# K loads on a second queue in a planned attention and feed-forward kernel

## The chip, the core and the metric

The kernel runs on one core of one Trainium2 chip. A core has five engines that each work through their own list of instructions in order: TensorE (PE in the profile) multiplies matrices, ScalarE (ACT) evaluates functions such as exp and tanh, VectorE (DVE) does elementwise arithmetic, GpSimd (POOL) does casts here, and SyncE (SP) only issues transfers. They meet through semaphores. Transfers between the chip's memory and the core's on-chip memory (SBUF) run on 16 DMA engines; SP, ACT and POOL each have a queue into them. Matmul results land in PSUM, eight banks of 2 KB per partition.

The metric is the time of one execution on the device, in microseconds (us), as the median of several runs.

## The reference

Eight batches of eight heads, 576 positions, head size 64: blockwise causal attention with blocks of 64, and then, on its 4608 rows of 512, a feed-forward layer with the activation h·sigmoid(beta·h).

```python
scores = scale * q @ k.T                      # per batch and head, 576 x 576
scores = where(pos_i // 64 >= pos_j // 64, scores, -1e9)
attn = softmax(scores)
x = (attn @ v).transpose(0, 2, 1, 3).reshape(4608, 512)
h = x @ w_in                                  # 512 -> 2048
g = h * (1 / (1 + exp(-beta * h)))
out = g @ w_out                               # 2048 -> 512
```

All inputs and the output are float32. The kernel multiplies in bf16 and f16.

## The kernel before, in words

**Attention.** The work is cut into 32 units, `u = 4*b + c`: batch `b`, pair of heads `c`. A unit needs Q and K with the head dimension on the partitions (`QKT`), so Q and K are loaded (`ST`), cast to bf16 on POOL (`QKn`) and transposed. For batches 0 and 1 a pair's Q and K come in small loads (L606), and PE transposes them (L622, copied out by DVE at L630). From batch `QB = 2` on, all of a batch's Q is one load and all of its K another (L641, 1.18 MB each), each into one of the two big buffers of class `S8`; POOL casts them in four pieces each (L653), and two DMA transposes (L660), one for each two pairs, write `QKT`. Then PE forms the transposed scores (L692), two heads at once on two halves of the array ("row" mode), ACT takes exp into `E` (L706, L718), DVE clears the masked corners (L712, L714), PE multiplies by V with a column of ones beside it (L744, "AV" below), and DVE divides by the sum (L756, L763). The result `xq` is transposed into `xT`, by PE and a copy for batches 0 to 2 (L783, L791, L793), by DMA from batch 3 on (L770). V comes in six loads a batch (L536, L539) into one buffer `Vs` and is cast by POOL (L562).

**Feed-forward.** It goes by nine blocks of 512 rows. For each of 16 columns of tiles, PE multiplies `xT` by `w_in` (L955, four matmuls a group), ACT takes tanh (L965) and DVE combines them into `gT` (L969). Block 0 then multiplies by `w_out` plainly (L991, 64 matmuls of 512 columns). The other blocks use Strassen's seven products (L885). ACT and DVE move the results to `ost`, and ACT issues the stores (L910, L1012).

**Weights.** POOL issues four loads of `w_in` (L490) and four of `w_out` (L495), which cast on the way. All four loads of `w_out` wait for the V of batch 1.

**What sets the order.** All of this is written as operations with a cost, dependences, buffers and a priority, and the class `Plan` orders them before the program is built: it simulates the five engines, PSUM banks and buffers, and the order in which its operations start becomes each engine's list of instructions. On the chip only the order is left, with the waits that `assign` derives. The plan's time for a load is `xfer` (what it would take alone), shared among queues that are active at once in proportion to `pkt`. It knows two queues before: "H" for all that SP and ACT issue, in one line, and "S" for POOL (L104 to L112). A list `seq` (L805 to L816) gives the loads on SP an order, through `after`; most of them are `lazy`, held back while over 3 us of load are queued.

Where PE would be idle in the plan's first 50 us, the plan puts in matmuls on a constant (fills, L511 in full mode, L513 as pairs in row mode). They read nothing that the kernel needs and keep PE busy. Their planned cost is 215 ns for the first 12 and 110 ns after.

Of the kernel before, what the change touches and what calls it, by code (L numbers as in the profile page):

```python
# [4 lines left out]
ACT = mybir.ActivationFunctionType  # L5
# [43 lines left out]
class Plan:  # L49
# [33 lines left out]
    def schedule(self):  # L83
# [20 lines left out]
        rings, left, clock = {"H": [], "S": []}, {"H": 0.0, "S": 0.0}, 0.0  # L104
        told, late = None, []

        def speeds():
            if rings["H"] and rings["S"]:
                h, w = rings["H"][0].pkt, rings["S"][0].pkt
                both = self.BOTH if clock > self.FIRST else self.BOTH0  # L110
                return {"H": h / (both * (h + w)), "S": w / (both * (h + w))}
            return {"H": 1.0, "S": 1.0}  # L112
# [56 lines left out]
        while nsched < len(self.ops) - len(fill) or pend or rings["H"] or rings["S"] or late:  # L169
# [26 lines left out]
            while progress:  # L196
                progress = False
                for e in engs:
# [62 lines left out]
                    if o.dma is not None:  # L261
                        x = "S" if e == "POOL" else "H"
                        left[x] += o.xfer
                        full = max(0.0, left[x] - self.RING) if e == "SP" else 0.0
                        o.todo = o.xfer
                        if x == "S":
                            at = now + (self.LATE if now > self.FIRST else self.LATE0)
                            late.append((at, o))
                            heapq.heappush(events, at)
                        else:  # L270
                            rings[x].append(o)
                        flow(now)
# [82 lines left out]
def bass_blockwise_causal_attn__then__act_swish_beta_kernel(  # L355
# [10 lines left out]
    with es:  # L366
# [138 lines left out]
        for i in range(NFILL):  # L505
            tf = P.tile("P1")

            def ff(g, e, tf=tf, i=i):
                o = fills[i]
                if o.mode == "full":  # L510
                    return g.matmul(PS[:, tf.slot, 0:256], identB[:], identW)  # L511
                for r in (slice(0, 64), slice(64, 128)):
                    z = g.matmul(PS[r, tf.slot, 0:256], identB[r, r], identW[r, :])  # L513
                return z

            n = 215 if i < 12 else 110
            o = P.op("PE", n, ff, deps=[c2, c4], tiles=[tf], lat=n, mode="full", prio=1e6 + i)
            o.fill = TFILL
            fills.append(o)
# [4 lines left out]
        for b in range(B):  # L524
# [4 lines left out]
            for h0, h1, e, tt in PARTS[b]:  # L529

                vs = []
                for i in tt:
# [10 lines left out]
                    if e == "SP":  # L543
                        o = P.op("SP", 300 + 550 * n, fv, tiles=[ts], xfer=(1400 if b == 0 else 1580) * n,
                                 prio=3.5 + 0.1 * (h0 > 0) if b == 0 else 4 * b + (3.5 if b < 2 else 0.5),
                                 dma=["d_V", h0, 1])
                    else:
# [40 lines left out]
        QKI, QKX = 1000, 5400  # L588
        for u in range(NU):
# [44 lines left out]
            elif p == 0:  # L634

                for w, (nm, src) in enumerate((("Q", q), ("K", k))):
                    if c == 0:
                        ts = whole[w] = P.tile("S8")

                        def fl(g, e, ts=ts, src=src, b=b):  # L640
                            return [g.dma_start(ST[ts.slot][:], src[b].rearrange("h t d -> (h t) d").rearrange(  # L641
                                "(i p) d -> p i d", p=128))]

                        o = P.op("SP", QKI, fl, deps=[o for t in early6 for o in t.users] if b == QB else [],
                                 tiles=[ts], xfer=QKX, prio=u, dma=["d_S8", 0, 1])
                        for i in range(NPAIR):
                            ld[nm, u + i] = o
                    ts, o = whole[w], ld[nm, u]
# [137 lines left out]
            xp = P.op("PE", 5 * 66, fx, deps=nrm, tiles=[tx, px], lat=5 * 66 + 170, mode="full", prio=pr(u)+.5 + 5 * (b < 1))  # L786

# [18 lines left out]
        for b in range(B):  # L806
            for u in range(4 * b, 4 * b + 4):
                for o in (ld["Q", u], ld["K", u]):
# [135 lines left out]
        for r in range(NRC):  # L944
# [37 lines left out]
            for w, d0, d1 in [(w, 0, DM) for w in range(4)]:  # L982
# [5 lines left out]
                for j0, j1 in parts:  # L988
# [12 lines left out]
                    o.after = was  # L1001
# [83 lines left out]
```

## Time and profile before

| | |
|---|---|
| median of 3 runs | 340.45 us (340.06 to 344.98) |
| span of the profiled run | 340.1 us |
| PE busy | 325.4 us (96%) |
| DVE, ACT, POOL busy | 220.9, 211.6, 83.0 us |
| DMA bytes | 53.41 MB, 157 GB/s over the span, 193 to 241 GB/s in most slices of the first 230 us |

The profile's page gives busy time by engine, then the span in 40 slices of 8.5 us with a digit for the busy tenths, then DMA by queue, the chain of work that ended last, and groups of instructions by source line. Beside it stand answers of the trace: the list of waits (who waited for whom, total, times, longest), the timeline (start, length, engine, line, operation, and in brackets the idle time before it and what ended it), and tables of windows. A PE duration is partly modelled, since matmuls are pipelined: eight matmuls of 256 columns follow each other at 109 ns although each is shown with a mean of 273 ns.

### The profile page before, as it was taken

What the parts mean: (1) busy time and instruction counts of PE and PEld (TensorE: products, weight loads), DVE (VectorE), ACT (ScalarE), POOL (GpSimd) and SP (SyncE); (2) the same over time, 40 slices, a digit from 0 to 9 for tenths busy, and PEclk for the clock granted to TensorE, in tenths of its full rate; (3) what the DMA queues carried; (4) which work ended last, traced back from release to release, by engine and by line L of the source; (5) the groups of instructions that cost most, each with busy time, mean ns of one, the idle gap of its engine ahead of it and who ended that gap; (6) DMA issues with size and microseconds to landing.
All of it is one profiled execution on the core that took longest, in us unless ns stands there. A gap on an engine that the chain in (4) does not pass through costs nothing.

```text
span 340.1 us, 7452 instructions
## 1 busy us (share of the span) xinstructions
PE 325.4 (96%) x3104; PEld 205.2 (60%) x3081; DVE 220.9 (65%) x447; ACT 211.6 (62%) x314; POOL 83.0 (24%) x127
## 2 busy tenths in 40 slices
PE   7798999999998999999999999999999999999995
PEld 5366446544685546754665676466656766666684
DVE  4718768479663687547976685657566766666742
ACT  1861993268645886777687747877677545544511
POOL 7665180316414400432035124303000000000000
PEclk9879999999999999999999999999999999999999
DMA  8999899999999595999889979994221200110023
GB/s 218 220 238 234 169 234 241 230 230 227 210 199 227 137 212 115 193 195 213 176 176 206 207 172 242 193 207 116 72 60 22 81 32 33 39 56 31 18 78 123
DMA packets 113313, 53.41 MB, mean 157 GB/s; under 512 B 83568, under 2 KB 112768, under 8 KB 113280
## 3 DMA queue, kind: packets, MB, share of 16 engines
q1 hardware_dynamic: 98432, 39.14, 57.7%
q10 hardware_dynamic: 9280, 9.44, 9.0%
q0 software_dynamic: 5568, 4.36, 8.1%
q8 instruction: 24, 0.39, 0.5%
q14 instruction: 9, 0.07, 0.1%
HBM read 36.71 MB, written 9.44 MB: 136 GB/s over the span
## 4 chain that ended last, share of the span: by engine, by line
PE 83%; ACT 9%; DVE 5%; issue 2%; POOL 0%; POOLq 0%; ACTq 0%
PE PS L955 31%; PE PS L885 28%; PE PS L744 7%; PE PS L692 7%; ACT E L706 5%; PE PS L991 4%; ACT th L965 3%; DVE gT L969 2%; PE PS L511 2%; PE PS L513 2%; PE PS L783 1%; PE PS L622 1%; DVE xq L763 1%; DVE QKT L630 1%; DVE QKn L613 0%
## 5 line engine op out<-in xcount | busy, mean ns | idle before, releaser
L955 PE MATMUL PS<-xT,w_in 128*128 128x512 bf16 x543 | 131.1, 380 | 3.2 <-ACT xT L791 0.4
L965 ACT ACTIVATE th<-PS,beta 128x512 f32<-128x512 f32 x144 | 96.6, 695 | 60.1 <-PE PS L955 59.7
L969 DVE SCALAR_TENSOR_TENSOR gT<-th,PS 128x512 f16<-128x512 f32 x144 | 95.7, 682 | 37.9 <-ACT th L965 37.4
L706 ACT ACTIVATE E<-PS 128x1024 bf16<-128x1024 f32 x93 | 92.0, 1027 | 32.8 <-PE PS L692 32.7
L955 PEld LDWEIGHTS PS<-xT,w_in 128*128 128x128 bf16 x576 | 52.9, 98 | 57.4 <-issue 2.7
L885 PE MATMUL PS<-w_out,gT 128*128 128x256 f16 x512 | 63.9, 273 | 0.3 <-ACT ost L900 0.3
L885 PEld LDWEIGHTS PS<-w_out,gT 128*128 128x128 f16 x512 | 48.6, 98 | 12.4 <-issue 0.4
L653 POOL CAST QKn<-ST 128x640 bf16<-128x640 f32 x48 | 35.7, 744 | 46.8 <-DMA ST<-in_k_dram 25.7
L562 POOL CAST Vn<-Vs 128x640 bf16<-128x640 f32 (+1 forms) x28 | 20.9, 747 | 93.6 <-DMA Vs<-in_v_dram 92.3
L692 PE MATMUL PS<-QKT 64*64 64x64 bf16 (+4 forms) x328 | 37.8, 303 | 0.4 <-ACT E L706 0.3
L744 PEld LDWEIGHTS PS<-Vn,E 128*128 128x128 bf16 x930 | 31.4, 97 | 7.0 <-DVE E L712 1.5
L744 PE MATMUL PS<-Vn,E 128*128 128x65 bf16 x930 | 32.6, 193 | 2.4 <-DVE E L712 1.2
L885 PE MATMUL PS<-OV 128*128 128x256 f16 x256 | 32.1, 273 | 0.0
L900 ACT ACTIVATE ost<-PS 128x512 f32<-128x512 f32 x32 | 19.2, 601 | 20.6 <-PE PS L885 20.2
L692 PEld LDWEIGHTS PS<-QKT 64*128 64x128 bf16 (+1 forms) x328 | 13.6, 97 | 26.8 <-issue 14.3
L885 PEld LDWEIGHTS PS<-OV 128*128 128x128 f16 x256 | 24.3, 98 | 5.8 <-issue 0.4
L763 DVE TENSOR_TENSOR xq<-PS,inv 128x640 bf16<-128x640 f32 x32 | 26.3, 821 | 0.7
L903 DVE SCALAR_TENSOR_TENSOR ost<-PS,ost 128x512 f32<-128x512 f32 x24 | 16.4, 688 | 13.0 <-PE PS L885 8.3
L712 DVE MEMSET E<- 64x64 uint32 x62 | 6.9, 112 | 25.8 <-ACT E L706 24.1
L852 DVE TENSOR_TENSOR OV<-gT 128x1024 f16<-128x1024 f16 x32 | 22.8, 727 | 0.4
L885 PE MATMUL PS<-OV,gT 128*128 128x256 f16 x128 | 15.9, 273 | 0.0
L991 PE MATMUL PS<-w_out,gT 128*128 128x512 f16 x64 | 15.2, 380 | 0.0
(60 smaller groups left out, 175.4 us busy)
## 6 DMA issues: line engine op xcount, KB each, us to landing
out_dram<-ost ACTq DMA_DIRECT2D x36, 256.0 KB, 2.8
Vs<-in_v_dram SPq DMA_DIRECT2D x24, 256.0 KB, 4.9
ST<-in_q_dram SPq DMA_DIRECT2D x8, 288.0 KB, 6.8
ST<-in_k_dram SPq DMA_DIRECT2D x8, 288.0 KB, 6.9
w_in<-in_moe_w_in_dram POOLq DMA_DIRECT2D x4, 512.0 KB, 10.7
w_out<-in_moe_w_out_dram POOLq DMA_DIRECT2D x4, 512.0 KB, 11.7
OV<-in_v_dram SPq DMA_DIRECT2D x4, 256.0 KB, 10.2
Vs<-in_v_dram SPq DMA_DIRECT2D x6, 128.0 KB, 8.0
```

The costliest lines, as they stand in the source:

```text
L562: return g.tensor_copy(Vn[t.slot][:, 0:n, g0:g1, 0:64], Vs[ts.slot][:, 0:n, g0:g1, :])
L653: return g.tensor_copy(QKn[tn.slot][:].rearrange("p a w n -> p (a w n)")[:, 640 * (2 * a + w):][:, 0:640] .rearrange("p (t h d) -> p t h d ...
L692: z = g.matmul(o, QKT[tqk.slot][r, p, 1, 128 * t + y:128 * t + m + y], x)
L706: return g.activation(E3[es_(te)][:, g0, :, :], PS[:, ps.slot:ps.slot + 2, :], ACT.Exp, scale=0.125)
L744: z = g.matmul(o, eblk(te, t, i, h), Vn[Tv.slot][:, t, 2 * c + h, 0:65], start=(t == 0), stop=(t == i))
L763: return g.tensor_tensor(xq[tx.slot][:].rearrange("p i (h d) -> p h i d", h=2), both(pv, 0, 64), x, ALU.mult)
L852: return P.op("DVE", dve_t(SZ * HC / 2), mk(lambda g: g.tensor_tensor(fo(), fx(), fy(), op)), deps=deps, tiles=tiles, prio=prio)
L885: x = g.matmul(PS[:, ps.slot, HM * w:HM * w + HM], fa()[:, j, 128 * w:128 * w + 128], fb()[:, j, :], start=first and w == 0 and j == 0, st ...
L955: z = g.matmul(PS[:, ph.slot, :], w_in[:, c, 128 * j:128 * j + 128], xT[:, c, row % RX:row % RX + RC], start=(c == 0), stop=(c == 3))
L965: return g.activation(th[tt.slot][:], PS[:, ph.slot, :], ACT.Tanh, scale=beta[:, j:j + 1])
L969: return g.scalar_tensor_tensor(out=gT[tg.slot][:, j, :], in0=th[tt.slot][:], scalar=1.0, in1=PS[:, ph.slot, :], op0=ALU.add, op1=ALU.mult)
L991: z = g.matmul(PS[:, po.slot, 0:d1 - d0], gT[tg.slot][:, j, 128 * w:128 * w + 128], w_out[:, j, d0:d1], start=(j == 0), stop=(j == NJ - 1))
```

## The change

From batch 2 on K's load is issued by ACT, so it goes through ACT's queue, where before only the stores were. Q's load stays on SP. Three more things go with it.

- The planner gets a third queue, "A", for what ACT issues; three active queues share by `pkt`. An issue on ACT into a full queue now holds ACT in the plan.
- Loads get times and weights that were read from a trace: V from batch 1 on 1200 in place of 1580 for a full piece, with `pkt` 90 in place of 22 (for batch 0 too); Q and K 5900 in place of 5400, with 72 in place of 22. Fills cost 140 in place of 110 after the first 12.
- Of K's loads of batches 2 to 7, none is in `seq` any more: each may go once Q of its batch has started in the plan, and none is lazy. Q always takes buffer 0 and K buffer 1. The plain products with `w_out` of rows 256 to 511 of block 0 may start, in the plan, only after the last PE transpose of batch 1 (`turn`).

What is computed is the same. Since the order of nearly everything follows from the plan, the lists of all engines change. PE's list in the changed kernel has 29 fills in full mode and 38 half-array ones, against 32 and 68; it changes into row mode 59 times against 56. The last part, from the last AV on, is the same matmuls in the same order.

```diff
-        rings, left, clock = {"H": [], "S": []}, {"H": 0.0, "S": 0.0}, 0.0
+        rings, left, clock = {"H": [], "A": [], "S": []}, {"H": 0.0, "A": 0.0, "S": 0.0}, 0.0
...
         def speeds():
-            if rings["H"] and rings["S"]:
-                h, w = rings["H"][0].pkt, rings["S"][0].pkt
-                both = self.BOTH if clock > self.FIRST else self.BOTH0
-                return {"H": h / (both * (h + w)), "S": w / (both * (h + w))}
-            return {"H": 1.0, "S": 1.0}
+            p = {k: r[0].pkt for k, r in rings.items() if r}
+            both = 1.0 if len(p) < 2 else self.BOTH if clock > self.FIRST else self.BOTH0
+            return {k: p[k] / (both * sum(p.values())) if k in p else 1.0 for k in rings}
...
-                        x = "S" if e == "POOL" else "H"
+                        x = {"POOL": "S", "ACT": "A"}.get(e, "H")
                         left[x] += o.xfer
-                        full = max(0.0, left[x] - self.RING) if e == "SP" else 0.0
+                        full = max(0.0, left[x] - self.RING) if x != "S" else 0.0
...
-            n = 215 if i < 12 else 110
+            n = 215 if i < 12 else 140
...
-                        o = P.op("SP", 300 + 550 * n, fv, tiles=[ts], xfer=(1400 if b == 0 else 1580) * n,
+                        o = P.op("SP", 300 + 550 * n, fv, tiles=[ts], xfer=(1400 if b == 0 else 1200) * n,
                                  prio=3.5 + 0.1 * (h0 > 0) if b == 0 else 4 * b + (3.5 if b < 2 else 0.5),
                                  dma=["d_V", h0, 1])
+                        o.pkt = 90.0
...
-        QKI, QKX = 1000, 5400
+        QKI, QKX = 1000, 5900
...
                         ts = whole[w] = P.tile("S8")
+                        ts.only = (w,)
...
-                        o = P.op("SP", QKI, fl, deps=[o for t in early6 for o in t.users] if b == QB else [],
+                        o = P.op("ACT" if w else "SP", QKI, fl, deps=[o for t in early6 for o in t.users] if b == QB else [],
                                  tiles=[ts], xfer=QKX, prio=u, dma=["d_S8", 0, 1])
+                        o.pkt = 72.0
                         for i in range(NPAIR):
                             ld[nm, u + i] = o
+                        if w:
+                            o.after = ld["Q", u]
...
+            if u == 2 * NPAIR - 1:
+                turn = xp
...
-                for o in (ld["Q", u], ld["K", u]):
+                for o in (ld["Q", u], ld["K", u])[:2 if b < QB else 1]:
...
-                    o.after = was
+                    o.after = was or (turn if w > 1 else None)
```

More of the change, by code (lines that the diff above doesn't have):

```diff
@@ L168, in schedule @@
         fill = [o for o in self.ops if o.fill]
-        while nsched < len(self.ops) - len(fill) or pend or rings["H"] or rings["S"] or late:
+        while nsched < len(self.ops) - len(fill) or pend or any(rings.values()) or late:
             if not events:
```

## The prediction

> **What bounds the kernel now.** I read the page first, then the windows, then the timelines of PE, SP and POOL where PE loses time. The page:
>
> ```profile
> PE 325.4 (96%) x3104; PEld 205.2 (60%) x3081; DVE 220.9 (65%) x447; ACT 211.6 (62%) x314; POOL 83.0 (24%) x127
> ...
> PE   7798999999998999999999999999999999999995
> ...
> ACT  1861993268645886777687747877677545544511
> ...
> DMA  8999899999999595999889979994221200110023
> ```
>
> PE is the bound: 96% busy, and the other engines have room. The DMA engines are nearly full for the first 230 us, but PE hardly waits for them, since feed-forward work fills the time of attention. From 264 us on there is only that work; both kernels have the same matmuls there, in the same order. So a load that lands earlier gains nothing by itself. Only time that PE loses can be won: waits, fills, and changes between array modes. The windows say where it is lost (columns: busy us of PE, PEld, DVE, ACT, POOL with counts, granted clock, DMA share, GB/s):
>
> ```profile
> 17.00:25.00 8.00, 8.00 (x99) 5.07 (x98) 1.36 (x7) 5.64 (x7) 5.23 (x8) 0.74 1.14 240
> 25.00:34.00 9.00, 7.87 (x168) 6.30 (x163) 7.77 (x17) 1.61 (x5) 5.11 (x8) 1.00 1.20 233
> 34.00:52.00 18.00, 17.16 (x136) 7.99 (x131) 12.84 (x27) 17.32 (x27) 9.38 (x13) 1.00 1.00 203
> 52.00:82.00 30.00, 29.71 (x249) 15.09 (x244) 21.05 (x44) 14.90 (x23) 6.35 (x9) 1.00 1.11 233
> 82.00:100.00 18.00, 17.84 (x215) 11.97 (x211) 12.65 (x30) 12.96 (x20) 6.53 (x8) 1.00 1.08 214
> 100.00:130.00 30.00, 28.60 (x275) 16.14 (x267) 19.56 (x47) 22.19 (x34) 8.64 (x12) 1.00 0.88 187
> 130.00:160.00 30.00, 28.84 (x338) 19.53 (x332) 17.12 (x40) 20.18 (x30) 8.64 (x12) 1.00 0.95 181
> ```
>
> PE idles 1.13 us in 25 to 34, 0.84 in 34 to 52, 0.45 in the next two together, 1.40 and 1.16 in the last two. Idle time is not all of it: from 17 to 25 PE is busy without a gap, but with what? DVE works 1.36 us there. The timeline of PE:
>
> ```profile
> 21.31 1.06 PE L513 MATMUL PS<-identF,identB 64*64 64x256 bf16 x16
> 22.31 0.39 PE L692 MATMUL PS<-QKT 64*128 64x64 bf16 x4
> 22.63 0.95 PE L513 MATMUL PS<-identF,identB 64*64 64x256 bf16 x14
> 23.51 0.39 PE L692 MATMUL PS<-QKT 64*128 64x320 bf16 x4
> 23.84 0.84 PE L513 MATMUL PS<-identF,identB 64*64 64x256 bf16 x12
> 24.61 1.98 PE L744 MATMUL PS<-Vn,E 128*128 128x65 bf16 x60
> ```
>
> Fills, and AV of the first two units behind them. POOL's timeline has the casts of their V from 19.12 for 1.50, so done by 20.6. AV stood ready for 4 us behind fills that the plan had put there for a V it expected later. ACT then has 1.61 us of work from 25 to 34, and 17.32 of 18 from 34 to 52: idle first, the limit after.
>
> For K, the timeline of SP and the issues by line:
>
> ```profile
> 40.20 0.75 SPq L641 DMA_DIRECT2D ST<-in_q_dram  x1
> 41.40 4.29 SPq L641 DMA_DIRECT2D ST<-in_k_dram  x1
> 45.74 17.74 SPq L536 DMA_DIRECT2D Vs<-in_v_dram  x4
> 63.53 7.14 SPq L660 DMA_TRANSPOSE QKT<-QKn  x2
> ```
>
> ```profile
> L641 SPq DMA_DIRECT2D ST<-in_q_dram x6: 719/726/751, 40.2 to 200.2; - x6
> L641 SPq DMA_DIRECT2D ST<-in_k_dram x6: 722/4284/4435, 41.4 to 208.0; - x6
> ```
>
> K's issue holds SP for 4.28 us (min/median/max in ns) where Q's takes 0.73: it finds the queue full of Q. V's four issues then hold SP until 63.5, and only then do the transposes go. POOL waits 25.7 us in all for K, six times (the list of waits). PE does not wait for any of it.
>
> [...] the DMA row is full with one load queue and POOL's, [...] No row of before shows two such queues with large loads from SP and ACT; SP and POOL together do: K of batch 2, issued at 41.40, is cast from 59.62 on, with three loads of `w_out` issued meanwhile. [...]
>
> **The change part by part.**
>
> *K's issue on ACT.* SP loses six issues of 4.28 us in the median; no engine but SP was held by them. ACT gains six: at least 0.73 + 0.37 us (Q's issue and the shape move before it, same listing), together 6.6 us, with an empty queue. If ACT's queue were as full as SP's was, 4.3 us each, 26 us. I take the low end: ACT's queue otherwise holds stores of 256 KB, which were issued in 0.38 us even at 174.9, while SP stood in a K issue. ACT is 62% busy, so most of the 6.6 us lie in its idle time; I charge PE a tenth, 0.6 us, with both ends 0 and 3.
>
> *The wait that comes with it.* Each of the six issues waits for POOL's casts of the K before. Behind it in ACT's list stand exp and tanh, and PE waits for those within a few us, as scores and `w_in` products share eight PSUM banks. The list puts the first issue after exps of batch 1, when POOL's last cast (33.88 + 0.82 before) should be just done, and the others one batch's work, some 30 us, apart, while K's casts follow its landing at once. I take 0 and keep 2 us each, 10 in all, for a rival.
>
> *Fewer fills and an earlier AV.* Before, 34 half-array pairs cost 6.1 us in the groups by line, 0.18 each. The pairs planned at 140 are 19. In the timeline, 13 of the old pairs lie before 21 us at about 0.22 (half clock) and 21 after it in 2.65 us; of the new ones 10 lie before (2.2 us in place of 2.86) and 9 after at some 0.15 (1.35 in place of 2.65). That is 2.0 us. One group of scores, 0.4, also moves behind the first AV, which can then start at about 22.3 in place of 24.6. Its V is cast by 20.6, so nothing else holds it. The transposes and scores of batch 1 follow some 4 to 5 us earlier than the 33.7 of before, into ACT's idle stretch, since POOL's list has three of their casts before two issues of `w_in` (1.48 us) that were ahead of them.
>
> How much of it lasts? The next gate is V of batch 1. It was waited for by POOL until 41.9, and K of batch 2 now starts at about 36 and shares with it for its last 5 us: some 3 us later, 44 to 45. Its casts, 0.77 each, follow the first `w_out` issue (0.74), so AV of batch 1 can start at about 46. At the same amount of PE work before had reached 51.35 less 16 matmuls of `w_in` at 0.216, or 47.9. So 1.9 us last if this gate binds, 5 if it doesn't. I take 3.0.
>
> *Fewer waits from 100 us on.* The two windows 100 to 160 idle 2.56 us, of which about 0.2 per 20 us is unavoidable by the later windows, so some 1.4 us are to be had there, and as much may lie in gaps too short for the row. A plan that has its load times from measurement puts work where its inputs really are, and K arrives with Q. I take 1.5 of it, between -3 (new misplacements, since a list is fixed) and +6.
>
> *Three more changes into row mode.* Before a group of scores the trace shows "issue" gaps, 14.3 us in 58 of them, 0.25 each: +0.75.
>
> *`turn`, buffers, `seq`, V's times.* They reorder work that is done anyway; no cost.
>
> Sum: 0.6 - 3.0 - 1.5 + 0.75 = -3.15, so 340.45 goes to **337.3 us**.
>
> **The rivals.** *A, the middle empties too:* with Q and K together, scores never wait, and the start keeps its 5 us: 0 - 5 - 4 + 0.75 = -8, 332.4. For it: 25.7 us of POOL's waits for K. Against: PE is at 99% from 52 to 100 already, and DMA is as full as before. *B, the transfer was hidden anyway:* the start's gain is lost at V of batch 1 and at `w_out`, all of it on full DMA engines: 0.6 - 0.5 - 0.5 + 0.75, or 340.8, no change. For it: the DMA row. Against: before, PE at 24 us waited for its own list, not for a load. *C, ACT is held:* 10 us from POOL's casts, 0.6 for issues, 0.75, with 3 won at the start: +8.4, 348.8, slower. For it: ACT at 17.32 of 18 us just where the first K is issued. Against: POOL is idle three quarters of the time.
>
> **How the numbers follow.** Forecast 0.52, A 0.22, B 0.18, C 0.08. The range from 331.8 to 342.5 holds the forecast with its bounds, A and B, and leaves C and the far end of A. Faster by over 2% means below 333.6: A, and a little of the forecast, 0.23. Slower by over 2% means above 347.3: most of C, 0.06. The rest, 0.71, is within.
>
> **What would show it.** In the changed kernel: the first AV at 22 to 23 us, the half-array fills at about 3.6 us in place of 6.1, and PE's idle time in 25 to 52 smaller than 1.97. K's issues on ACT near 0.73 us, with the wait ahead of them near nothing. K's casts no longer long after Q's. PE's idle time in 100 to 160 below 2.6. The forecast is wrong if ACT stands before a K issue while PE waits for exps, if AV of batch 1 waits for V beyond 48, or if the first scores of batch 2 wait for their transposes by several us.

## The result and the profile after

The changed kernel takes 365.74 us in the median of 4 runs (364.09 to 367.67), the kernel before, beside it, 342.72 (340.06 to 345.20, 4 runs): 1.070 times as long, with a 95% interval of 1.057 to 1.084. The forecast was 337.3, with a range of 331.8 to 342.5. Ratios, here and below, compare only the runs in the faster of the two states that the executions of one kernel fall into, so a ratio can differ from that of the medians beside it. The span of the profiled run grew from 340.1 to 362.3 us. Page of the changed kernel:

```profile
PE 332.3 (92%) x3104; PEld 205.7 (57%) x3048; DVE 218.2 (60%) x447; ACT 211.0 (58%) x320; POOL 82.4 (23%) x127
...
PE   7879959876998999999956999999999999999996
...
PEclk9999969996999999999995999999999999999999
DMA  8999999999999599999799786150231021020023
```

PE's row has three holes: a 5 in the sixth slice, a 7 and a 6 in the ninth and tenth, a 5 and a 6 in the 21st and 22nd. PEclk, the granted clock, drops to 5 or 6 in or just behind each of them. From 200 us on PE has no such hole. The windows (columns as before):

```profile
17.00:25.00 8.00, 6.49 (x121) 4.49 (x117) 3.44 (x12) 4.20 (x6) 5.20 (x8) 1.00 0.98 234
...
34.00:52.00 18.00, 12.99 (x113) 6.79 (x108) 9.68 (x20) 11.14 (x18) 3.77 (x6) 0.91 1.13 220
52.00:82.00 30.00, 26.52 (x206) 13.19 (x199) 15.38 (x33) 9.63 (x15) 10.67 (x15) 0.94 1.16 206
82.00:100.00 18.00, 15.35 (x124) 6.86 (x123) 10.14 (x22) 13.98 (x22) 8.91 (x12) 0.81 1.12 218
100.00:130.00 30.00, 29.08 (x311) 19.35 (x301) 17.29 (x43) 17.08 (x28) 8.64 (x12) 1.00 0.88 187
130.00:160.00 30.00, 29.07 (x324) 17.71 (x315) 19.96 (x45) 22.46 (x34) 6.10 (x8) 1.00 1.06 214
...
180.00:200.00 20.00, 13.16 (x110) 7.56 (x107) 8.89 (x19) 8.59 (x16) 3.22 (x4) 0.74 1.10 211
```

PE's idle time is 5.0 us in 34 to 52 (0.84 before), 3.5 in 52 to 82 and 2.7 in 82 to 100 (0.45 for both before), 6.8 in 180 to 200. The timeline of PE names the waits, in brackets:

```profile
20.13 1.08 PE L747 MATMUL PS<-Vn,E 128*128 128x65 bf16 x30 [0.50 <-POOL Vn L561]
...
49.57 2.65 PE L747 MATMUL PS<-Vn,E 128*128 128x65 bf16 x45 [4.57 <-POOL Vn L561]
...
84.43 1.89 PE L960 MATMUL PS<-xT,w_in 128*128 128x512 bf16 x4 [4.73 <-ACT ost L1011]
...
193.24 1.83 PE L747 MATMUL PS<-Vn,E 128*128 128x65 bf16 x30 [6.84 <-DMA xT<-xq]
```

The first AV stands at 20.13 us instead of 24.61. Most of that distance is not the change: in the profiled execution of before PE had half clock from 14.3 to 21.1 us. h1 below has the list of before on PE, and its profiled execution had no half clock there; its timeline of PE has this AV at 21.17:

```profile
21.17 1.98 PE L744 MATMUL PS<-Vn,E 128*128 128x65 bf16 x60
```

So at full clock the new list gains 1.0 us. With half clock early in both (h2 below has the new list and half clock from 12.1 to 19.0) it gains 2.7, with the AV at 21.93 against 24.61.

Then PE waits 4.6 us for V of batch 1, 4.7 for ACT and 6.8 for a DMA transpose. The timelines of SP and then of ACT show what stood where:

```profile
34.37 3.62 SPq L534 DMA_DIRECT2D OV<-in_v_dram  x1
38.04 1.64 SPq L537 DMA_DIRECT2D OV<-in_v_dram  x2
40.14 0.75 SPq L641 DMA_DIRECT2D ST<-in_q_dram  x1
```

```profile
37.44 0.86 ACTq L641 DMA_DIRECT2D ST<-in_k_dram  x1
...
75.64 0.60 ACT L1011 ACTIVATE ost<-PS 128x512 f32<-128x512 f32 x1 [1.04 <-PE PS L996]
76.50 0.69 ACT L970 ACTIVATE th<-PS,beta 128x512 f32<-128x512 f32 x1 [0.27 <-PE PS L960]
76.50 7.23 ACTq L1017 DMA_DIRECT2D out_dram<-ost  x1
83.78 0.60 ACT L1011 ACTIVATE ost<-PS 128x512 f32<-128x512 f32 x1 [6.59 <-issue]
```

K is issued at 37.44, just ahead of the two last, small pieces of V of batch 1 (38.04). By the trace's landings these took 8.7 us each (2.9 and 2.5 before) and landed at 46.8 and 47.8, K itself at 47.5: the pieces came in together with K, and V was there at 47.8 instead of 41.6. At 76.50 a store's issue stands 7.23 us on ACT, with K, issued at 73.97, ahead of it in the same queue. At 185.13 the transposes of `xT` were issued 0.5 us after K (184.65); they took 8.1 us and landed at 193.2, again behind K (192.7). K's own issue costs what was forecast, and waits for nothing:

```profile
L641 ACTq DMA_DIRECT2D ST<-in_k_dram x6: 712/732/946, 37.4 to 184.7; - x6
L641 SPq DMA_DIRECT2D ST<-in_q_dram x6: 726/732/751, 40.1 to 191.2; - x6
```

**A balance.** The trace records each change of the granted clock. Leaving out the last stretch of each kernel, which begins in the last 2 us of the span or behind it, the changed kernel has half clock in three stretches, 48.7 to 55.5, 82.8 to 89.6 and 188.6 to 198.8 us; before has one, 14.3 to 21.1. Half a clock for t us is counted here as a loss of t/2, an estimate (30 matmuls of an AV took 1.08 us at 20.13 and 1.83 at 193.24). The gaps are those of over 1.5 us between the starts of two matmuls, from 25 us on. Without both, the spans of the kernels that are needed below lie at 333 to 336 us, and at 339 to 340 for two of them:

| kernel | span | gaps | half clock | span - gaps - half clock/2 |
|---|---|---|---|---|
| before | 340.1 | 1.5 | 6.8 | 335.2 |
| after | 362.3 | 17.2 | 23.9 | 333.2 |
| e1, planned anew with K on SP | 350.7 | 6.5 | 10.2 | 339.1 |
| e6, before with the new times | 346.9 | 3.6 | 6.8 | 339.9 |
| h1, list of before, K on ACT | 357.9 | 19.1 | 10.2 | 333.7 |
| h2, list of after, K on SP | 360.4 | 14.3 | 20.5 | 335.9 |
| h3, h1 with stores on POOL | 349.5 | 11.6 | 6.8 | 334.5 |
| b2, list of before, two edits | 335.9 | 1.5 | 0 | 334.4 |

So what the change lost are a few long waits of PE and the half clock behind them: 17.2 + 11.9 = 29.1 us against 4.9. What it won, some 2 us of the rest, is small beside that. e1 and e6 lose more than the table's waits: gaps of 0.6 to 1.5 us add up to 10 to 12 us over the span in the four kernels of the table whose list was planned with the new times, and to 4 to 6 in the others. The experiments ask where the waits come from.

### The profile page after: what moved, and what is told of

It is laid out like the page before. It is cut to its first block, busy times and chain, and to the rows that moved or that the text cites. A ratio compares the mean times of both kernels' runs of the same rounds, so it can differ in the third digit from the quotient of the medians.

```text
span 362.3 us, 7406 instructions
## 1 busy us (share of the span) xinstructions
PE 332.3 (92%) x3104; PEld 205.7 (57%) x3048; DVE 218.2 (60%) x447; ACT 211.0 (58%) x320; POOL 82.4 (23%) x127
## 4 chain that ended last, share of the span: by engine, by line
PE 69%; DVE 6%; SPq 6%; DMA 6%; ACT 4%; POOL 3%; ACTq 3%; issue 2%; POOLq 0%
PE PS L960 28%; PE PS L890 24%; PE PS L747 7%; SPq L534 5%; PE PS L695 5%; PE PS L996 4%; DVE gT L974 3%; ACTq L1017 2%; DMA OV<-in_v_dram 2%; DMA xT<-xq 2%; ACT E L709 2%; DMA Vs<-in_v_dram 1%; DVE xq L766 1%; DVE OV L857 1%; ACT th L970 1%
## 5 line engine op out<-in xcount | busy, mean ns | idle before, releaser
L960 PE MATMUL PS<-xT,w_in 128*128 128x512 bf16 x576 | 143.3, 388 | 5.2 <-ACT ost L1011 4.7
L747 PE MATMUL PS<-Vn,E 128*128 128x65 bf16 x930 | 35.2, 198 | 12.2 <-DMA xT<-xq 6.8
L747 PEld LDWEIGHTS PS<-Vn,E 128*128 128x128 bf16 x930 | 33.5, 101 | 17.8 <-DMA xT<-xq 7.1
L695 PE MATMUL PS<-QKT 64*128 64x512 bf16 (+4 forms) x328 | 37.6, 300 | 2.3 <-ACT E L709 2.0
L695 PEld LDWEIGHTS PS<-QKT 64*128 64x128 bf16 (+1 forms) x328 | 13.5, 96 | 30.1 <-issue 13.8
L759 DVE RECIPROCAL inv<-PS 128x10 f32<-128x10 f32 x32 | 6.9, 217 | 18.9 <-PE PS L747 18.6
L996 PE MATMUL PS<-w_out,gT 128*128 128x512 f16 x64 | 16.3, 395 | 0.0
```

Of the source, the lines that this page charges most:

```text
L695: z = g.matmul(o, QKT[tqk.slot][r, p, 1, 128 * t + y:128 * t + m + y], x)
L747: z = g.matmul(o, eblk(te, t, i, h), Vn[Tv.slot][:, t, 2 * c + h, 0:65], start=(t == 0), stop=(t == i))
L960: z = g.matmul(PS[:, ph.slot, :], w_in[:, c, 128 * j:128 * j + 128], xT[:, c, row % RX:row % RX + RC], start=(c == 0), stop=(c == 3))
L996: z = g.matmul(PS[:, po.slot, 0:d1 - d0], gT[tg.slot][:, j, 128 * w:128 * w + 128], w_out[:, j, d0:d1], start=(j == 0), stop=(j == NJ - 1))
```

## The experiments

There were three theories at first. "One line": loads of SP and ACT move in the order in which they are handed over, while the plan lets them share. "Sharing": they share. "Constants": the new times make a list that fits badly whatever the queue.

### The loads alone

A kernel of loads and stores only: nothing is computed, and most of the output is not written. Each case ran twice in one execution, and the two agree within 0.3 us in each landing.

> Only loads and stores, nothing is computed and most of the output is not written. Twice through five cases, each begun when all before has landed: Q (1.18 MB) from SP and K from ACT at once; K from ACT, then V's two last pieces (64 KB each) from SP; Q from SP, then two stores (256 KB) from ACT; K from POOL, then the pieces from SP; K from ACT, then two stores from ACT. Theory one line: of Q and K at once one lands after some 8 us and the other after 13; the pieces from SP land only with K from ACT, some 8 us after their issue, but after 3 to 5 us beside K from POOL. Theory sharing: Q and K both land after 12 to 13 us, and the pieces after 3 to 5 us in both cases. A store behind K in ACT's own queue is held 3 us or more at its issue under both.

Its timeline (first the case of K and small pieces, then that of K and a store on one queue):

```profile
15.35 0.70 ACTq L81 DMA_DIRECT2D SK<-in_k_dram  x1
16.09 0.20 ACT L82 ACTIVATE w<-w 128x1 f32<-128x1 f32 x1 [0.78 <-issue]
16.39 1.36 SPq L72 DMA_DIRECT2D VS<-in_v_dram  x2
23.91 0.20 ACT L85 ACTIVATE w<-w 128x1 f32<-128x1 f32 x1 [7.62 <-DMA VS<-in_v_dram]
...
43.27 0.70 ACTq L81 DMA_DIRECT2D SK<-in_k_dram  x1
44.02 0.20 ACT L82 ACTIVATE w<-w 128x1 f32<-128x1 f32 x1 [0.78 <-issue]
44.09 4.39 ACTq L87 DMA_DIRECT2D out_dram<-STO  x1
```

Two pieces of 64 KB, handed over by SP 1 us after K on ACT, land 7.2 and 6.7 us later, right behind K (8.0). With K from POOL, and the pieces 2.2 us after it, the same (7.6 and 7.2). Q and K handed over in the same instant share: 11.3 and 13.2 us. A store right behind K on ACT stands 4.39 us in its issue, 4.68 the second time; one beside Q on the other queue 0.36. So "one line" holds for these small pieces behind a load that was already handed over, by POOL too, which neither theory had expected; "sharing" for two handed over together.

This is no rule for all transfers. Two stores that ACT issued 0.0 and 0.4 us after Q on SP landed after 2.5 and 5.2 us, well ahead of Q (8.2). In the kernel before, the first two loads of `w_out` that POOL issued after K of batch 2 landed at 50.8 and 55.6 us, K at 59.6.

### The list planned anew

**e1**: K back on SP and in `seq`; the third queue (for stores), the times and `turn` stay.

```diff
-                        o = P.op("ACT" if w else "SP", QKI, fl, ...
+                        o = P.op("SP", QKI, fl, ...
-                for o in (ld["Q", u], ld["K", u])[:2 if b < QB else 1]:
+                for o in (ld["Q", u], ld["K", u]):
```

> The changed kernel with K of batches 2 to 7 issued by SP again and in the list of loads; the planner's third queue (now for stores alone) and all new times stay, and everything is planned anew. Theory one line (loads that SP and ACT issue are moved in the order of issue, while the plan lets them share, so K on ACT goes ahead of V's last pieces and of later stores): V of batch 1 lands by 42 us, PE has no wait of over 2 us after 40 us, the clock stays full; 335 to 343 us. Theory sharing (K takes a fair third of the DMA engines, and the extra load is what delays V): the same, 335 to 343. Theory constants (the new times and weights give a list that doesn't fit, whatever the queue): 355 or more.

Measured: 352.59 us, ratio 1.035 (1.028 to 1.041). Between the two expectations: with K on SP, over 3% are still lost.

**e6**: before with the new times alone.

```diff
-            n = 215 if i < 12 else 110
+            n = 215 if i < 12 else 140
...
-                        o = P.op("SP", 300 + 550 * n, fv, tiles=[ts], xfer=(1400 if b == 0 else 1580) * n,
+                        o = P.op("SP", 300 + 550 * n, fv, tiles=[ts], xfer=(1400 if b == 0 else 1200) * n,
...
+                        o.pkt = 90.0
...
-        QKI, QKX = 1000, 5400
+        QKI, QKX = 1000, 5900
...
+                        o.pkt = 72.0
```

> The kernel before, K on SP and its plan of one load line, with the changed kernel's load times alone: half-array fill 140 instead of 110, V 1200 with weight 90 instead of 1580 with 22, Q and K 5900 with weight 72 instead of 5400 with 22. Theory 'times': the new times by themselves make a list that fits the loads worse, then 350 to 356, as when K was put back on SP with the rest of the change kept (352.6). Theory 'queue': the new times fit as well as the old ones and only a plan that lets two queues share is wrong: 335 to 344.

Measured: 348.73 us, 1.026 (1.023 to 1.029). The new times by themselves cost 7.8 to 9.9 us, more than "queue" allowed and a little less than "times" asked. Of it the timeline of PE shows one long wait, with 3.4 us of half clock behind it; the rest is in shorter gaps, which were not followed one by one:

```profile
172.46 1.05 PE L887 MATMUL PS<-w_out,gT 128*128 128x256 f16 x8
176.88 1.42 PE L957 MATMUL PS<-xT,w_in 128*128 128x512 bf16 x4 [3.37 <-DMA xT<-xq]
```

These transposes were issued at 167.12, right behind Q (166.35) on SP, and took 9.4 us. In before they are no faster (8.4 us for those behind Q and K of the same batch), but PE's list comes to them later: among its waits there is none for a DMA.

**e7**: before's single line and old times, with K on ACT.

```diff
-                        o = P.op("SP", QKI, fl, ...
+                        o = P.op("ACT" if w else "SP", QKI, fl, ...    # only=(w,), after Q, not in seq
```

> The kernel before with K on ACT alone: issued behind Q as in the change, but planned with the old times, in the old single line with SP's loads, stores too, and ACT charged only for its issue. Theory 'K on ACT costs by itself': stores behind K hold ACT for 3 to 8 us and later small loads wait for K, so 350 to 362 although the plan's times are old. Theory 'plan': with the old times and no sharing between SP and ACT assumed, the list fits: 336 to 345.

Measured: 362.07 us (355.72 to 368.58), 1.048 (1.042 to 1.053). As "K on ACT costs by itself" has it, though in the profiled run ACT was held only 5.8 us in two issues. The larger part were waits of up to 2.6 us between 101 and 124 us, with 20.5 us of half clock, whose cause was not followed further.

**e2** and **e8** give the planner the order that the loads alone showed. e2 puts ACT into SP's line; e8 keeps the three queues and serves, of SP's and ACT's loads, only the one handed over first.

```diff
# e2
-                        x = {"POOL": "S", "ACT": "A"}.get(e, "H")
+                        x = "S" if e == "POOL" else "H"
# e8, in speeds()
+            last = max((k for k in "HA" if k in p), key=lambda k: rings[k][0].start, default=None)
+            if "H" in p and "A" in p:
+                p.pop(last)                 # its speed: 1e-9
...
```

> The changed kernel, K still issued by ACT, but planned as if SP and ACT fed one line (as in the kernel before). Theory one line: the plan now knows that V's last pieces wait for K, and that an issue behind K holds ACT, so it puts other work there; the waits of 4.6, 4.7 and 6.8 us shrink to under 2 each, and it runs in 337 to 346 us. Theory sharing: the plan is now wrong about the queues and the waits stay or grow; 360 or more. Theory constants: 355 or more.

> The changed kernel with one thing altered in its planner: while SP's and ACT's queue both hold a load, the one handed over first is served alone and the other waits, as the loads alone did on the chip; POOL's queue shares as before. Theory 'sharing was assumed': the list that comes out has its loads where they land, 340 to 352, with what is left of the loss in ACT's stores behind K. Theory 'any list of this kind misfits': 358 or more.

Measured: 373.75 us, 1.096 (1.089 to 1.102), and 366.61, 1.078 (1.068 to 1.089). Both miss what "one line" and "sharing was assumed" asked (337 to 346 and 340 to 352) and lie where their rivals put them (360 or more, 358 or more). So "the plan assumed sharing" falls as the whole cause. What both plans still lack is the held store: behind a K the plan charges a store's issue 5.9 + 0.9 - 6.0 = 0.8 us at most (its load, its own, less the 6 us that it takes a queue to hold), where the chip took 3.1 to 8.2 in the changed kernel and h1. In e2 five issues held ACT for 28.2 us, in e8 the two longest for 7.2. e2 also charges ACT for what SP has queued, so it is no clean test.

**e3**: K of batch 2 also waits for V of batch 1.

```diff
+                            o.deps += ld["V", 1, 0] if b == QB else []
```

> The changed kernel in which only K of batch 2 also waits for the landing of V of batch 1; planned anew. Theory one line: V lands by 42 us, the first AV of batch 1 waits under 1 us and the clock stays full until 80 us, so 4.6 us of wait and about 3.4 us of half clock go: 354 to 359 us. Theory sharing: V lands 3 us earlier, of which 3 us are won: 360 to 363. Theory constants: within 2 us of 364.

Measured: 371.18 us, one run, above all that was expected (354 to 366). The first wait is gone, but the new list has others, 8.1 us in two and one of 7.5, all for ACT, which two store issues held for 11.7 us. Whatever is planned anew mixes its own waits with those of the edit. The rest therefore keep a list and change single places in it.

### The list of the changed kernel, kept

**f1** moves K of batch 2 behind V's small pieces, **f3** the early stores from ACT's list to POOL's, **f4** does both and moves K of batch 7 behind the transposes. **e4** puts 40 useless matmuls of 256 columns into PE's list right before its wait for the V of batch 1.

```diff
         P.schedule()
+        later(ld["K", 4 * QB], 5)           # f1, f4: five places later in ACT's list
+        later(ld["K", 28], 4)               # f4
+        for o in [o for o in P.order["ACT"] if o.dma and o.dma[0] == "d_ost" and o.start < 135e3]:
+            P.order["ACT"].remove(o)        # f3, f4: to POOL's list, by planned time
...
```

> The changed kernel's lists are kept as they are, instruction for instruction; only the first K on ACT (batch 2) is issued five ACT instructions later, so that the two last pieces of V of batch 1 (64 KB each) are handed over first. Theory 'queue ahead': those pieces were late only because a load of 1.18 MB had been handed over before them. Then V of batch 1 lands near 42 instead of 47.8, the first stall of PE (4.6 us) and the half clock after it (6.83 us at half speed, worth 3.4) go: 365.7 - 8.0, some 358 us. Theory 'list that fits nothing': PE takes the saved time up again at other waits in the next 30 us, the time stays above 362. Theory 'fair share': the pieces land no earlier, 365 us.

> The changed kernel's lists, with one edit: the eight stores of the first output rows (planned before 135 us) are issued by POOL instead of ACT, at the same planned place; K stays on ACT. Theory 'ACT held': the store's issue stood 7.2 us in ACT because K lay ahead in the same queue, and PE waited 4.9 us for ACT. Without a store behind K on ACT this stall and its half clock (6.83 us, worth 3.4) go: 365.7 - 8.3, some 357 us; ACT's longest issue in 70 to 130 us falls below 1 us. Rival: the stores land as late as before (K is ahead of them on the DMA engines), the output tiles come free as late, and PE waits for them all the same: above 362.

> The changed kernel's lists with three edits: the K of batch 2 five ACT instructions later, the K of batch 7 four ACT instructions later (behind the DMA transposes of xT that PE waited 7.0 us for), and the eight early stores on POOL. If the three stalls with the half clock after each are the whole loss: 365.7 - (4.6 + 3.4) - (4.9 + 3.4) - (7.0 + 5.1), or 337 us, as forecast for the change itself, and no stretch of half clock after 21 us. If the list as a whole fits the loads badly, PE waits elsewhere: 345 to 355.

> The changed kernel with 40 matmuls without use (256 columns, 0.11 us each at full clock, 4.3 us) put into the wait of PE for V of batch 1 (4.6 us in the changed kernel); everything else as it was. It separates the wait from the clock after it. If the half clock at 48.7 to 55.5 comes from the idle PE, it goes, and with it 6.83/2 = 3.4 us: 362.3. If the clock has another cause, the time stays at 365.7 and the half clock stays.

f1: 361.61 us, 1.053 (1.045 to 1.061); its four runs took 357.6, 358.6, 364.6 and 367.6, and the lower two are what "queue ahead" asked. In the profiled one, the longest of the four, the pieces landed at 42.3 and 42.8 us, 2.9 and 2.6 after their issue, and PE has no gap of over 1.5 us between 25 and 75 us: the cause of the first wait is shown. f3: 361.87, 1.066 (1.058 to 1.073), next to the rival's "above 362". The longest store issue on ACT fell below 1 us, and no wait of PE for ACT is left among its seven longest; but PE then waited 9.6 us at 153 for transposes issued 0.2 us after a K. f4: 359.06, 1.054 (1.047 to 1.062), far from 337 and above the 345 to 355 of its rival. It has a new wait, here in its timeline of PE:

```profile
94.76 1.89 PE L996 MATMUL PS<-w_out,gT 128*128 128x512 f16 x8
102.06 0.80 PE L695 MATMUL PS<-QKT 64*128 64x320 bf16 x6 [5.41 <-DMA QKT<-QKn]
```

These transposes were issued at 91.35, K on ACT 1 us after them, and they took 10.7 us. So in f3 and f4 PE, with earlier waits taken away, stood at the next load that K had delayed.

e4: 359.71, 1.060 (1.052 to 1.067). Its clock row, against that of the changed kernel shown above:

```profile
PEclk9998999999999989999996999999999999999999
```

The 6 in the sixth slice is gone with the fills in the wait, so that half clock did come from the idle PE. (The 8 in the fourth slice is a new stretch of 3.4 us at 26 us, ahead of the edit.) The time fell by 1.0% of before, about the 3.4 us expected; as other waits moved too and the intervals overlap, that sum is not shown by it alone.

### Two lists, two queues

**h1**: the list of before, with K's six loads moved from SP's list to ACT's at the same planned time. **h2**: the list of after, with them moved to SP's list behind their Q. Nothing is planned again.

```diff
         P.schedule()
+        for o in dict.fromkeys(ld["K", 4 * b] for b in range(QB, B)):      # h1
+            P.order["SP"].remove(o)
...
+            L = P.order["ACT"]
+            L.insert(next((i for i, x in enumerate(L) if x.start > o.start), len(L)), o)
```

> The list of before, instruction for instruction, with the six loads of K from batch 2 on taken out of SP's list and put into ACT's at the same planned time; nothing is planned again. Theory 'queue': stores and later small loads behind K cost by themselves, whatever the list: 350 to 360, with ACT held over 3 us in some store issues. Theory 'list': the old list has work where its inputs land, and V, now handed over right behind Q, lands no later than before: 337 to 345, and the loss of the change is that of the new list.

> The list of the changed kernel, instruction for instruction, with the six loads of K put back into SP's list right behind their Q; nothing is planned again. Theory 'queue': ACT's stores are not held any more, V of batch 1 is handed over ahead of K, and two of the three stalls go: 345 to 352. Theory 'list': V and the transposes on SP now stand behind K too and come later still, so 360 or more.

| | K on SP | K on ACT |
|---|---|---|
| list of before | 1 | 1.057 (1.047 to 1.067) |
| list of after | 1.059 (1.050 to 1.067) | 1.070 (1.057 to 1.084) |

Each alone costs nearly all of it: "queue" is right for h1 (361.06 us, just above its 350 to 360), "list" for h2 (362.35). Both run a list that was planned for the other queue, so part of each loss may be that misfit; plans that knew K's place still lost: 1.048 with K on ACT and the old times (e7), 1.035 with K on SP and the new ones (e1). In h1, the timeline of ACT and then that of PE:

```profile
176.15 0.72 ACTq L641 DMA_DIRECT2D ST<-in_k_dram  x1
...
178.41 8.16 ACTq L910 DMA_DIRECT2D out_dram<-ost  x1
186.61 1.02 ACT L706 ACTIVATE E<-PS 128x1024 bf16<-128x1024 f32 x1 [7.61 <-issue]
```

```profile
179.68 1.02 PE L955 MATMUL PS<-xT,w_in 128*128 128x512 bf16 x4
187.69 0.80 PE L692 MATMUL PS<-QKT 64*128 64x320 bf16 x6 [6.98 <-ACT E L706]
```

Three such issues (4.82, 8.16 and 7.08 us) hold the exps behind them, and PE waits 13.8 us for exps in all. In h2 it is another wait, by its list of waits, with no ACT in it:

```profile
PE PS L747 <- DMA xT<-xq: 12.1, 6, 3.7
PE PS L695 <- DMA QKT<-QKn: 3.4, 2, 2.6
```

### What K on ACT costs in the list of before

**h3**: h1 with the stores planned before 240 us on POOL. **h5**: h3 with K of batch 5 six, and of batch 7 three instructions later in ACT's list.

```diff
+        later(ld["K", 20], 6)               # h5
+        later(ld["K", 28], 3)
```

> The list of before with K on ACT (as run: 361.1 us), and the stores planned before 240 us moved from ACT's list to POOL's at the same planned time, so that none stands behind K on ACT. If the held ACT is the whole loss: 340 to 346, with PE's waits for exps (13.8 us in four) nearly gone. If two queues with loads cost by themselves: 352 or more, with PE waiting for transposes or for V instead.

> The kernel with the list of before, K on ACT and the early stores on POOL (352.9 us), with two of the six K loads some 4 us later in ACT's list: that of batch 5 six instructions later and that of batch 7 three, so that the transposes of xT, which SP begins to issue 0.9 and 2.5 us before those K, are handed over whole before K is. If K passing them is the rest of the loss, they land some 4 to 8 us sooner, the waits at 146 and 214 us (4.6 and 5.4) and the half clock after them (3.4 each, worth 1.7) go: 352.9 - 13.4, or 339.5, the time of before. If PE then waits for K's own casts instead: 346 or more.

h3: 352.94 us, 1.035 (1.027 to 1.043), as "two queues with loads cost by themselves" has it. PE's waits for exps are nearly gone (0.3 us), and 2.2% with them. What is left is of another kind. The timelines of SP, ACT and PE in h3, and then that of SP in before, around Q and K of batch 5:

```profile
136.19 0.73 SPq L641 DMA_DIRECT2D ST<-in_q_dram  x1
138.03 7.64 SPq L770 DMA_TRANSPOSE xT<-xq  x3
```

```profile
138.91 0.69 ACTq L641 DMA_DIRECT2D ST<-in_k_dram  x1
```

```profile
145.30 1.04 PE L885 MATMUL PS<-OV,gT 128*128 128x256 f16 x8
150.69 1.89 PE L955 MATMUL PS<-xT,w_in 128*128 128x512 bf16 x4 [4.36 <-DMA xT<-xq]
```

```profile
136.16 0.72 SPq L641 DMA_DIRECT2D ST<-in_q_dram  x1
140.04 2.30 SPq L770 DMA_TRANSPOSE xT<-xq  x1
143.22 0.75 SPq L641 DMA_DIRECT2D ST<-in_k_dram  x1
```

In before SP issues K only after the transpose, which lands at 146.4 (6.3 us). In h3 K goes from ACT while SP still stands in the transpose's issue; K lands at 150.1 and the transpose at 150.6 (12.6 us). At 204 it is the same, 15.2 us. h5 puts K of batch 5 behind it; its timelines of SP and ACT:

```profile
139.12 9.16 SPq L770 DMA_TRANSPOSE xT<-xq  x3
```

```profile
147.39 0.72 ACTq L641 DMA_DIRECT2D ST<-in_k_dram  x1
```

The first of these transposes lands at 147.7 (8.6 us), and the wait at 146 us is gone. The K of batch 7 was moved too little (issued at 208.62, with the transposes' issue going on until 210.69): they still took 14.9 us, and PE waited 2.9. It also waited 2.2 us for transposes at 176, where it had not in h3. Time: 347.41 us, 1.013 (1.003 to 1.024), where 339.5 was expected. So of the 5.7% of h1, 2.2 go with the stores off ACT and 2.2 with the two K issued later. Of the 1.3 that remain, with an interval that nearly reaches 0, these two waits are the part that the trace shows.

### What became of the earlier start

**b1**: before, with all but the first 14 half-array pairs left out of PE's list. **b2**: b1, with Q of batch 7 behind the transposes issued next. **h4**: b2 with K on ACT and the stores on POOL, as in h3.

```diff
         P.schedule()
+        cut = [o for o in P.order["PE"] if o.fill and o.mode != "full"][14:]   # out of PE's list
+        L = P.order["SP"]; i = L.index(ld["Q", 28]); L.insert(i + 1, L.pop(i))   # b2
```

> The kernel before with its lists kept and only the last half-array fills left out (all but the first 14 pairs), so that AV of the first units can start about 2 us earlier, at 22.5 instead of 24.6. If the early start lasts, 338; if it ends at the wait for V of batch 1 or of w_out, 340.5, the same. Above 343 only if the clock falls after 24 us because PE waits there with nothing to do.

> The kernel before with fewer half-array fills, as run already, and Q of the last batch behind the DMA transposes of xT that were issued next after it on SP, nothing else. In the run with fewer fills alone those transposes took 10.7 us to land, PE waited 3.6 us for them at 207 us and worked at half clock for 3.4 after it. If a load ahead is what delayed them, they land in about 4 us, this wait goes and the early lead lasts: 336 to 338, 1% faster than before. If something else takes the lead: 340 to 341.

> The kernel that beat before (fewer fills, Q of the last batch behind the transposes; 339.2 us), with K on ACT and its early stores on POOL. If K on ACT is neutral once nothing stands behind it: 338 to 341. If the sooner V and transposes are worth something: 335 to 337. If the loss has a second part: above 345.

b1: 341.56 us, 1.001 (0.997 to 1.004), no difference. Its first AV is at 19.61, where the same list with all its fills has it at 21.17 at full clock (h1) and at 24.61 in the profiled execution of before. At 206.56 us b1 leads that execution by 3.5. Its timeline of PE there:

```profile
206.56 1.08 PE L744 MATMUL PS<-Vn,E 128*128 128x65 bf16 x30
211.24 3.26 PE L955 MATMUL PS<-xT,w_in 128*128 128x512 bf16 x8 [3.60 <-DMA xT<-xq]
```

Before has the same AV at 210.08 and the group after it at 211.51. In both kernels the transposes for this group were issued behind Q of batch 7 and landed near 211.2: the lead of 3.5 us shrinks to 0.3, and 3.4 us of half clock after the wait take more than the rest. Since most of this lead is the half clock that before had at its start, the two traces show how a lead ends at a landing that both lists meet at the same time, not what the fills are worth. With Q one place later (b2) they are issued at 198.95 and land in 3.4 us:

```profile
206.21 1.08 PE L744 MATMUL PS<-Vn,E 128*128 128x65 bf16 x30
207.12 1.89 PE L955 MATMUL PS<-xT,w_in 128*128 128x512 bf16 x8
```

b2: 339.15 us (337.45 to 340.20, 17 runs), 0.992 (0.989 to 0.995): faster than both kernels, by 1.9 to 3.9 us over before, a little short of the 336 to 338 expected. Q moved without the fills cut was not run, so how the gain divides between the two edits is not known. h4: 344.65, 1.010 (1.004 to 1.017), just short of "a second part". K on ACT makes the best list worse too, with a wait of 3.1 us for transposes at 146 as in h3.

## Why the prediction was wrong, point by point

- **"K's issue on ACT"**: the issue's own size was right, 0.73 us each, with nothing waited for. The step that failed most plainly is "I take the low end: ACT's queue otherwise holds stores of 256 KB, which were issued in 0.38 us even at 174.9, while SP stood in a K issue." That row shows a store on one queue and K on the other. The change puts both on one: up to 8.2 us for a store (4.4 in the loads alone), during which no exp or tanh starts. The term was 0.6 us with 3 at the most; in the list of before it was about 7.5 (h1 less h3, 2.2%).
- **"Fewer fills and an earlier AV"**: the AV was forecast 2.3 us earlier, and came 2.7 earlier where both executions had half clock at the start, but 1.0 at full clock. The half-clock stretch before 21 us, which the prediction read as part of the kernel before, belongs to that execution: three others with the same list (h1, h3, h5) did not have it. The half-array fills took 3.0 us (3.6 were forecast), against 6.1 in before and 4.7 in the same list at full clock.
- **"How much of it lasts?"**: wrong for the cause it names. It let K of batch 2 share with V of batch 1, "44 to 45"; it was 47.8, as two small loads that came 0.6 and 1.6 us after a load of 1.18 MB landed only with it, 8.7 us after their issue. No row of before had shown such sharing between SP and ACT; it was an assumption. The loads alone show it for two big ones handed over together (11.3 and 13.2 us), not for a small one behind a big one on another queue (7.2 us, where 2.9 were enough ahead of it in f1). As for the 3.0 us: in the list of before 1.9 to 3.9 us were to be had with fewer fills and one Q later (b2), not with fewer fills alone (b1).
- **"Fewer waits from 100 us on"**: the idle time in 100 to 160 did fall, from 2.56 to 1.85 us, in the two windows that the prediction looked at; but in 180 to 200, outside these two, PE idled 6.84 us, where it had 0.16 before. And -1.5 rested on "A plan that has its load times from measurement puts work where its inputs really are", while the new times alone cost 8.8 us (e6), above the +6 of its bound.
- **A term that the sum did not have**: the clock. Half clock entered it only in the price of fills. The half-clock stretches of the changed kernel last 6.83, 6.83 and 10.24 us, and each begins within a wait of PE of 4.6 to 6.8; by the estimate of the balance they cost about 11.9 us, half their length, beside 17.2 us of waits.
- **"The wait that comes with it"** and **rival C**: C said 348.8 for an ACT held by a wait for casts. ACT was held and that rival's side was the right one, but for another reason: there was no wait before K, the holding came after it.
- Of what would show it wrong, "if AV of batch 1 waits for V beyond 48" came true to the letter (49.57), and PE's idle time in 25 to 52, to be below 1.97, was 5.97 us.
- Two slips in the working change nothing in this. POOL issued four loads of `w_out`, not three, between K's issue at 41.40 and its cast at 59.62, and rival A's terms add up to -8.25, so 332.2.

What stays open: how the 1.059 of the new list with K on SP divides between its times, its order, `turn` and the fact that it was planned for K on ACT (e6 has 1.026 for the times in another list), and what else is in the last 1% of h5. The 0.75 us for more changes into row mode was not tested apart. The two causes do not add, 1.057 and 1.059 alone and 1.070 together; no run shows why. The likeliest reading, argued only, is that PE reaches a late transpose later when it has already lost time at a held ACT.

## What to carry to other kernels

In before, SP's 115 transfers landed in the order of their issue, but for one pair: the order of one list was the order of the landings. Before a big load moves to another queue, list the small loads and transposes that its old place kept ahead of it and the instructions behind it on the new engine, and count on each of them waiting for the whole big load rather than for a share of it: here they landed 7 to 15 us after their issue. For a TensorE that is 96% busy, count each wait of over 2 us with the half clock that may follow it: here it lasted 3.4 us with a gap of 2.4 (h5) and 10.2 with one of 7.1 (the changed kernel). Judge a gain at the start only after finding the next wait that both lists meet at the same time, and compare two profiles only after looking at the clock of both.

## What the hardware showed that was not expected

- Two loads of 64 KB that SP issued 1.0 and 1.8 us after a load of 1.18 MB on another queue took 7.2 and 6.7 us, and 2.9 and 2.6 where they went first (f1). With the big load from POOL it is no different (7.6 and 7.2). But stores of 256 KB that ACT issued 0.0 and 0.4 us after such a load on SP landed after 2.5 and 5.2 us, ahead of it.
- A store of 256 KB behind such a load on its own queue held ACT 3.1 to 8.2 us (six issues in the changed kernel and h1), and 4.4 and 4.7 in the loads alone; beside a load on another queue its issue took 0.36.
- DMA transposes whose issue has begun can still be passed: K issued 0.9 us after the start of such an issue on SP landed first, and the transpose took 12.6 us (h3), against 8.6 with K behind it (h5) and 6.3 in before.
- Filling a wait of 4.6 us with useless matmuls removed 6.8 us of half clock after it (e4). In all full kernels of this study, every gap of over 4 us between the starts of two matmuls had half clock in or behind it (in the changed kernel 6.83, 6.83 and 10.24 us with gaps of 4.95, 5.11 and 7.12); of those of 2 to 4 us most had (2.4 us in h5 was followed by 3.4), some not (3.0 and 3.2 us in h1).
- One list can start with or without a stretch of half clock: 14.3 to 21.1 us in the profiled execution of before, none there in three others with the same list of PE. It moved the first AV by 3.4 us.
